# Attention with a learned position bias and a feed-forward layer on one core: bias rows 128 to 255 made per distance, constants in one load, two more places for the first layer

## The chip, the cores and the metric

The kernel runs on one core of a Trainium2 chip. The metric is the device time of one execution in microseconds (us). Engines are named as in the profile: PE is TensorE, DVE is VectorE, ACT is ScalarE, POOL is GpSimd, SP is SyncE, which here only issues transfers.

## What is computed

Batch 4, 8 heads, 576 positions, head size 64, all float32. To each head's scores a bias is added that a small network makes from the distance of the two positions; then softmax, the product with v, and a feed-forward layer (512 to 2048 to 512) over the 2304 tokens.

```python
scores = scale * np.matmul(q, k.transpose(0, 1, 3, 2))
rel = (pos[:, None] - pos[None, :]).astype(np.float32)
psi_rel = np.log1p(np.abs(rel))
psi_i = np.log1p(np.maximum(pos[:, None].astype(np.float32), 1.0))
x = (psi_rel / psi_i)[..., None]
h = np.maximum(x @ w1 + b1, 0.0)          # 32 hidden units
bias = h @ w2                             # 8 heads
scores = scores + bias.transpose(2, 0, 1)[None, :, :, :]
...                                       # softmax over the last axis
h = x @ w_in
g = h * np.clip(h + 3.0, 0.0, 6.0) / 6.0
out = g @ w_out
```

The bias doesn't depend on the batch, and the distance enters by its absolute value: row i of the bias needs h only for distances 0 to max(i, 575 - i).

## The kernel before

**The bias.** The 576 rows are made in 36 groups of 16 (`g`). In one group four rows of queries share a pass: 128 partitions are 4 rows times 32 hidden units, so a group has four first-layer passes (`z_group`, lines 1001 to 1022). A pass computes max(w1 * log-distance, -b1 * psi_i) or its Relu form, on ACT (line 1020) or on DVE (line 1016); groups below 16 alternate ACT and DVE, later ones have one ACT pass and three DVE passes. `T` holds the log-distances, already multiplied by w1 (lines 1243 to 1246, two DVE instructions). For groups below `EARLY = 16`, T is a table over signed offsets, and each pass reads a window of 576 columns of it. For later groups (`bias_far`) T is reloaded with one column per distance (`distances`, at tile 12), a pass reads only max(i, 575 - i) + 1 columns, and the row is unfolded on the way out of PSUM.

The second layer is a float32 matmul with `w2_sb` (line 1058; far groups line 1037), each pass on its own 32 of the output's partitions. ACT then scales by 1 / psi_i and adds a constant column of `cv_sb` (`bias_out`, line 1076): one instruction in an early group, two in a far one (the row to the right of the diagonal, and the mirrored row to its left). The group's rows go to a table in DRAM (line 1090, on ACT's queue), from which `load_bias` (line 645, on SP's queue) reads 128 rows for two heads at a time.

Passes of an even group write into `z_e`, of an odd group into `z_a`, in the first phase: each place is free again when its group's matmuls have read it. `z_a` also serves as the zeros for eight warm-up matmuls at the start (lines 1251 to 1255).

**The rest.** Around this, w_in and w_out are read as 64-bit floats in 1 MB pieces (line 396) and converted: ACT line 406, POOL line 407, DVE lines 414, 417 and 420 per piece, then the split in two halves, ACT line 285 and DVE line 302. Two buffers hold pieces of w_in, so a load waits until DVE line 420 has read the one before the last. The largest value of v is taken per 320 KB tile (DVE line 336). Score tiles follow as soon as their bias rows are in DRAM: scores on PE (line 683), with the bias added and the row's extreme taken on DVE (line 715), exp on ACT (line 726), transposes on PE (line 781). Feed-forward matmuls are lines 937 and 960.

**Order.** Every engine issues in program order, and `ISSUE` gives, for each engine, the order of its instructions as a list of their numbers in the order in which the kernel's Python creates them; what a list leaves out follows in that order. SP's numbers 0 to 7 are the constants' loads, then come w_in pieces, q/k tiles, v tiles and bias loads. All small loads, w_in, q, k, v and the bias loads stand in SP's one queue.

Of the kernel before, what the change touches and what calls it, by code (L numbers as in the profile page):

```python
# [1503 lines left out]
```

## Time and profile before

| what | value |
|---|---|
| median of 3 runs | 652.33 us (652.02 to 654.21) |
| the profiled execution | 653.62 us, of which its span 651.5 us |
| mean granted TensorE clock in it | 0.995 of full |
| busy share of the span: PE, PEld, ACT, DVE, POOL | 96%, 69%, 77%, 71%, 32% |

Busy time is what the profile counts for an engine's instructions; a share over the whole span is a mean over stages. Matmuls overlap, and their ends are modelled.

### The profile page before, as it was taken

What the parts mean: (1) busy time and instruction counts of PE and PEld (TensorE: products, weight loads), DVE (VectorE), ACT (ScalarE), POOL (GpSimd) and SP (SyncE); (2) the same over time, 40 slices, a digit from 0 to 9 for tenths busy, and PEclk for the clock granted to TensorE, in tenths of its full rate; (3) what the DMA queues carried; (4) which work ended last, traced back from release to release, by engine and by line L of the source; (5) the groups of instructions that cost most, each with busy time, mean ns of one, the idle gap of its engine ahead of it and who ended that gap; (6) DMA issues with size and microseconds to landing.
All of it is one profiled execution on the core that took longest, in us unless ns stands there. A gap on an engine that the chain in (4) does not pass through costs nothing.

```text
span 651.5 us, 14774 instructions
## 1 busy us (share of the span) xinstructions
PE 625.5 (96%) x5440; PEld 447.9 (69%) x5440; DVE 459.8 (71%) x1116; ACT 504.7 (77%) x993; POOL 208.3 (32%) x267
## 2 busy tenths in 40 slices
PE   6688998999999999999999999999999999999997
PEld 2225655666777777788888877777777777777775
DVE  4899999999858887676788667776677667821310
ACT  5898887999979989896799778976797678822620
POOL 0111115664223430452255125521444026300410
PEclk9889999999999999999999999999999999999999
DMA  8888788864679999999999999889878877640000
GB/s 278 317 322 298 283 310 318 308 232 140 163 205 247 215 274 194 264 251 234 257 259 248 203 209 180 176 177 205 173 142 187 181 168 139 113 81 21 1 12 31
DMA packets 176648, 130.57 MB, mean 200 GB/s; under 512 B 138304, under 2 KB 145728, under 8 KB 175552
## 3 DMA queue, kind: packets, MB, share of 16 engines
q1 hardware_dynamic: 166784, 114.14, 70.9%
q10 hardware_dynamic: 9792, 15.49, 8.5%
q8 instruction: 43, 0.70, 0.5%
q14 instruction: 29, 0.24, 0.1%
HBM read 77.54 MB, written 15.49 MB: 143 GB/s over the span
## 4 chain that ended last, share of the span: by engine, by line
PE 71%; DVE 4%; DMA 3%; ACT 1%; issue 0%; ACTq 0%; DVEq 0%; SPq 0%
PE o_ps L960 27%; PE h_ps L937 26%; PE s_ps L703 9%; PE pv_ps L868 6%; DMA at<-hl 2%; PE b_ps L1037 2%; DVE bt L715 1%; DMA wo<-in_w_out_dram 1%; DVE cu L420 1%; DVE cu L414 1%; ACT bt L726 0%; DVE wo L302 0%; PE pv_ps L822 0%; DVE cu L417 0%; ACT hl L285 0%
## 5 line engine op out<-in xcount | busy, mean ns | idle before, releaser
L937 PE MATMUL h_ps<-x,wi 128*128 128x256 f16 (+1 forms) x1536 | 205.7, 286 | 1.2 <-DVE x L1342 0.8
L960 PE MATMUL o_ps<-g,wo 128*128 128x256 f16 (+1 forms) x1536 | 198.8, 286 | 0.0
L937 PEld LDWEIGHTS <-wi 128*128 128x128 f16 x1536 | 146.6, 98 | 52.1 <-issue 15.8
L960 PEld LDWEIGHTS <-wo 128*128 128x128 f16 x1536 | 146.8, 98 | 46.4 <-issue 9.6
L916 POOL TENSOR_TENSOR g<-t,g 128x256 f16<-128x256 f32 (+1 forms) x128 | 105.0, 832 | 180.9 <-ACT g L914 173.9
L726 ACT ACTIVATE bt<-bt,sm 128x576 f32<-128x576 f32 x144 | 110.7, 770 | 31.0 <-DVE sm L715 30.6
L302 DVE SCALAR_TENSOR_TENSOR hl<-bt,sm,hl 128x576 f16<-128x576 f32 x112 | 95.2, 864 | 16.5 <-ACT hl L285 15.0
L285 ACT ACTIVATE hl<-bt,sm 128x576 f16<-128x576 f32 x112 | 84.0, 765 | 5.3 <-ACT bt L726 3.3
L920 DVE SCALAR_TENSOR_TENSOR t<-t,t,h_ps 128x320 f32<-128x320 f32 (+1 forms) x112 | 57.2, 516 | 40.2 <-ACT t L927 39.3
L564 POOL TENSOR_TENSOR qkl<-st,qkh 128x576 fp32r<-128x576 f32 (+2 forms) x48 | 53.1, 1124 | 90.3 <-ACT qkh L557 59.0
L914 ACT ACTIVATE g<-t 128x256 f16<-128x256 f32 (+1 forms) x128 | 54.9, 438 | 22.7 <-DVE t L920 22.3
L927 ACT ACTIVATE t<-h_ps,t,hr 128x320 f32<-128x320 f32 (+1 forms) x112 | 64.6, 586 | 8.4 <-PE h_ps L937 6.9
L715 DVE CUSTOM_DVE_ANT_0 bt<-s_ps,bt 128x576 f32<-128x576 f32 x88 | 64.8, 750 | 4.6 <-PE s_ps L703 4.4
L1016 DVE TENSOR_SCALAR z_e<-T,nbp 128x576 f32<-128x576 f32 (+17 forms) x76 | 36.5, 498 | 16.8 <-PE b_ps L1037 12.0
L734 DVE TENSOR_SCALAR sm<-sm 128x1 f32<-128x1 f32 x112 | 16.9, 151 | 44.0 <-ACT bt L726 43.7
L970 ACT ACTIVATE ot<-o_ps,os 128x256 f32<-128x256 f32 (+1 forms) x32 | 15.7, 491 | 38.4 <-PE o_ps L960 37.7
L1076 ACT ACTIVATE bo<-b_ps,cv_sb,isc 128x576 f32<-128x576 f32 (+36 forms) x60 | 36.7, 635 | 1.5 <-PE b_ps L1037 1.1
L715 DVE CUSTOM_DVE_ANT_0 bt<-s_ps,k 128x576 f32<-128x576 f32 x40 | 28.8, 752 | 5.9 <-PE s_ps L703 5.6
L407 POOL TENSOR_SCALAR w<-w 128x1024 f32<-128x1024 f32 x8 | 10.5, 1315 | 68.1 <-ACT wo L406 68.1
L868 PE MATMUL pv_ps<-at,vh 128*64 128x320 f16 (+1 forms) x432 | 32.0, 293 | 0.0
L1020 ACT ACTIVATE z_e<-T,bp 128x576 f32<-128x576 f32 (+17 forms) x36 | 24.9, 698 | 8.2 <-DVE bp L1247 3.4
L781 PE MATMUL t_ps<-eye_sb,bt 128*128 128x128 f32 x160 | 29.3, 280 | 1.1 <-ACT atf L784 0.5
(130 smaller groups left out, 845.0 us busy)
## 6 DMA issues: line engine op xcount, KB each, us to landing
bt<-bias SPq DMA_DIRECT2D x36, 576.0 KB, 5.6
w<-in_w_in_dram SPq DMA_DIRECT2D x8, 1024.0 KB, 6.6
vs<-in_vp_dram SPq DMA_DIRECT2D x24, 320.0 KB, 4.1
st<-in_qk_dram SPq DMA_DIRECT2D x16, 448.0 KB, 4.3
bias<-bo ACTq DMA_DIRECT2D x20, 295.5 KB, 4.4
wo<-in_w_out_dram SPq DMA_DIRECT2D x5, 1024.0 KB, 4.8
bias<-bo ACTq DMA_DIRECT2D x16, 288.0 KB, 4.3
bt<-bias SPq DMA_DIRECT2D x32, 144.0 KB, 3.3
```

The lines of the kernel that those rows point to most:

```text
L285: nc.scalar.activation(out=out, in_=full, func=AF.Copy, scale=scale)
L302: nc.vector.scalar_tensor_tensor(out=out, in0=full, scalar=scale, in1=high, op0=ALU.mult, op1=ALU.subtract)
L703: nc.tensor.matmul(out=s_t[n + j][:, a, 0:HALF], lhsT=w[q], rhs=m[rows, cs], start=(k == 0), stop=(k == 2),)
L715: nc.vector.tensor_tensor_reduce(out=halves(bt), in0=ps, in1=halves(src), op0=ALU.add, op1=ALU.min, scale=-0.125, scalar=3.0e38, accum_out ...
L726: nc.scalar.activation(out=bt, in_=bt, func=AF.Exp, scale=-1.0, bias=sm[:, 0:1], accum_out=total)
L868: nc.tensor.matmul(out=ps[64 * s:64 * s + 64, 0:n], lhsT=w[:, 128 * c + 64 * s:128 * c + 64 * s + 64], rhs=at[:, c, s * n:(s + 1) * n], st ...
L914: nc.scalar.activation(out=g[:, 0], in_=uu, func=AF.Copy)
L916: e.tensor_sub(out=g[:, 1], in0=uu, in1=g[:, 0])
L920: nc.vector.scalar_tensor_tensor(out=t_t[f], in0=t_t[f], scalar=cols(f)[2], in1=h_t.pop(f)[:, 0:n], op0=ALU.min, op1=ALU.mult,)
L927: nc.scalar.activation(out=t_t[f], in_=h_t[f][:, 0:n], func=AF.Relu, scale=cols(f)[0], bias=cols(f)[1],)
L937: nc.tensor.matmul(out=h_t[f][:, 0:n], lhsT=wi[:, a, c, f * 128:(f + 1) * 128], rhs=x[:, e, c], start=(k == 0), stop=(k == 3 * KC - 1),)
L960: nc.tensor.matmul(out=ops[:, 0:n], lhsT=wo[:, a, f, e * 128:(e + 1) * 128], rhs=g_t[f][:, r], start=(f == 0 and a == 0 and r == 0), stop= ...
```

## The change

- `EARLY` goes from 16 to 8, so groups 8 to 15 (rows 128 to 255) are made by `bias_far`, per distance. The DRAM table of rows 128 to 255 takes the shape that the tables of later rows have.
- T is no longer multiplied by w1. A pass does it: DVE's takes w1 and the bound as two scalars per partition, ACT's takes w1 as its scale. Two DVE instructions at the start and one POOL instruction in `distances` go.
- T's signed-offset part is columns 448 to 1147 and is loaded first; columns 0 to 447 hold distances from the start. `distances` loads only the other 128.
- w1, b1, psi, w2 and 1 / psi come in one block `cb`, in one load instead of five.
- `z_place`: groups 2, 3, 6, 7, 10 and 11 write their passes into two more places, in the buffers of the later transposed tiles (tags at0 and at1), so four places are in use up to group 11. The warm-up zeros move from `z_a` into a buffer of x.
- `s1` is 1: the constant columns `cv_sb` are made by six POOL memsets and one DVE multiplication, instead of a DVE memset and five DVE copies.
- All five issue lists are new. SP's starts: cb, T from 448 on, two v tiles, eye, a q/k tile, T up to 448, a q/k tile, w_in piece 0, a v tile, w_in piece 1, two q/k tiles, w_in pieces 2 and 3, the fourth v tile (number 18), the first bias load (12). DVE's starts: psi times b1, its negative, the zeros, three passes (groups 0, 1, 0), the maximum of the first v tile, a pass of group 3, `w2_sb` times 8 (number 4). PE's puts four of the eight warm-up matmuls behind the bias.

```diff
-EARLY = 16
+EARLY = 8
+ZMORE = 12
 LATE = 16 * EARLY
+FAR = 576 - LATE
...
-CFG = {... 's1': 0, ...}
+CFG = {... 's1': 1, ...}
...
 ISSUE = {
     "SP": """
-0-1 3 2 23 4 6 15 18 5 20 7 10 8 22 25 11-12 9 13-14 17 31 16 19 21 26 24 27-28 30 33 29 32 38 34 47
...
+0-1 11 14 2 6 3 7 4 16 5 8-10 13 18 12 19 17 15 22 21 20 26 23-24 27 25 29 28 30 43 32 31 35 33 47
...
+    cb = const.tile([128, 2 + S // 4 + 32 + NG], F32, name="cb")
+    w1_sb, b1_sb, bp = cb[:, 0:1], cb[:, 1:2], cb[:, 2:2 + S // 4]
+    w2_sb, isc = cb[:, 2 + S // 4:34 + S // 4], cb[:, 34 + S // 4:]
...
     def distances():
-        nc.sync.dma_start(out=T[:, 0:S], in_=dtab)
-        nc.gpsimd.tensor_scalar(
-            out=T[:, 0:S], in0=T[:, 0:S], scalar1=w1_sb, scalar2=1.0, op0=ALU.mult, op1=ALU.mult
-        )
+        nc.sync.dma_start(out=T[:, FAR:S], in_=dtab[:, FAR:S])
+
+    z_more = {}
+
+    def z_place(g):
+        if phase or g >= ZMORE or g % 4 < 2:
+            return z_a if phase == 0 and g % 2 else z_e
+        if g % 2 not in z_more:
+            t = at_p.tile([128, 5, 512], F32, tag=f"at{g % 2}", name="z_m")
+            t = t.rearrange("p a b -> p (a b)")[:, 0:4 * S]
+            z_more[g % 2] = t.rearrange("p (a b) -> p a b", a=2)
+        return z_more[g % 2]
...
-                z2 = (z_a if phase == 0 and g % 2 else z_e)[:, k // 2]
+                z2 = z_place(g)[:, k // 2]
...
-                    out=z, in0=src, scalar1=nbp[:, col], scalar2=None, op0=ALU.max
+                    out=z, in0=src, scalar1=w1_sb, scalar2=nbp[:, col], op0=ALU.mult, op1=ALU.max
...
-                nc.scalar.activation(out=z, in_=src, func=AF.Relu, bias=bp[:, col])
+                nc.scalar.activation(out=z, in_=src, func=AF.Relu, scale=w1_sb, bias=bp[:, col])
...
-    nc.sync.dma_start(out=T[:, 512:LT], in_=ltab[:, 512:LT])
-    nc.sync.dma_start(out=w1_sb, in_=w1c)
-    nc.sync.dma_start(out=b1_sb, in_=b1c)
-    (nc.scalar if cfg['s2'] else nc.sync).dma_start(out=bp, in_=psi)
-    nc.sync.dma_start(out=w2_sb, in_=w2b)
-    nc.sync.dma_start(out=isc, in_=ipsi)
+    nc.sync.dma_start(out=cb, in_=cblk)
+    nc.sync.dma_start(out=T[:, FAR:LT], in_=ltab[:, FAR:LT])
     nc.sync.dma_start(out=eye_sb, in_=eye)
-    nc.sync.dma_start(out=T[:, 0:512], in_=ltab[:, 0:512])
+    nc.sync.dma_start(out=T[:, 0:FAR], in_=dtab[:, 0:FAR])
...
-    for cs in (slice(512, LT), slice(0, 512)):
-        nc.vector.tensor_scalar(
-            out=T[:, cs], in0=T[:, cs], scalar1=w1_sb, scalar2=None, op0=ALU.mult
-        )
...
-        wz = z_a[:, 1, 0:S].bitcast(F16)
+        wz = x_p.tile([128, 2, KC, 256], F16, tag="x", name="wz")[:, 0].rearrange("p a b -> p (a b)")[:, 0:640]
```

## Rows read from the trace of the kernel before

**Rows 1.** Stretches: length, busy (xcount) of PE, PEld, DVE, ACT, POOL; clock, DMA share, GB/s.
```profile
5.00:53.00 48.00, 38.00 (x297) 15.00 (x297) 38.73 (x81) 41.38 (x57) 5.03 (x4) 0.93 0.89 315
53.00:150.00 97.00, 90.31 (x659) 58.17 (x661) 94.66 (x206) 83.00 (x154) 41.85 (x37) 1.00 0.80 294
150.00:200.00 50.00, 49.66 (x448) 35.88 (x447) 38.39 (x111) 44.21 (x88) 13.00 (x15) 1.00 0.65 171
200.00:600.00 400.00, 399.48 (x3689) 304.45 (x3688) 278.88 (x705) 318.08 (x663) 136.15 (x193) 1.00 0.91 192
```

**Rows 2.** The chain that ended last, around 160 us: start us, us, what.
```profile
159.54 0.76 DVE bt L715
...
160.36 0.44 PE t_ps L781 x2
```

**Rows 3.** DVE in order of time, the start: start us, us, what [idle before, releaser].
```profile
3.87 0.55 DVE L1244 TENSOR_SCALAR T<-T,w_sb 128x636 f32<-128x636 f32 x1 [3.87 <-DMA w_sb<-in_w1c_dram]
...
5.70 0.52 DVE L1016 TENSOR_SCALAR z_e<-T,nbp 128x576 f32<-128x576 f32 x1
```

**Rows 4.** ACT in order of time, the start.
```profile
5.42 1.44 ACT L1020 ACTIVATE z_e<-T,bp 128x576 f32<-128x576 f32 x2 [3.40 <-DVE bp L1247]
...
9.04 0.78 ACT L1020 ACTIVATE z_a<-T,bp 128x576 f32<-128x576 f32 x1 [1.51 <-PE w_ps L1255]
11.14 1.44 ACT L1020 ACTIVATE z_e<-T,bp 128x576 f32<-128x576 f32 x2 [1.32 <-PE b_ps L1058]
```

**Rows 5.** DMA issues of the first 60 us: median us from issue to landing at the end.
```profile
w<-in_w_in_dram SPq DMA_DIRECT2D x7, 1024.0 KB, 7.0
...
vf<-in_vp_dram SPq DMA_DIRECT2D x4, 320.0 KB, 5.6
T<-in_ltab_dram SPq DMA_DIRECT2D x1, 318.0 KB, 2.8
...
bp<-in_psi_dram SPq DMA_DIRECT2D x1, 72.0 KB, 2.4
```

**Rows 6.** Groups by line and shape, whole span: busy us, mean ns | idle before, releasers.
```profile
L1076 ACT ACTIVATE bo<-b_ps,cv_sb,isc 128x576 f32<-128x576 f32 x16 | 13.0, 824 | 0.3
L1020 ACT ACTIVATE z_e<-T,bp 128x576 f32<-128x576 f32 x17 | 12.8, 769 | 7.2 <-DVE bp L1247 3.4 <-PE b_ps L1058 2.9 <-ACT z_a L1020 0.8
...
L414 DVE TENSOR_SCALAR_CACHE_REDUCE cu<-cu 128x1024 f32<-128x1024 f32 x8 | 9.7, 1212 | 0.4 <-ACT cu L406 0.4
L1016 DVE TENSOR_SCALAR z_e<-T,nbp 128x576 f32<-128x576 f32 x19 | 9.4, 514 | 4.7 <-PE c_ps L1258 4.0 <-PE b_ps L1058 0.6
L1016 DVE TENSOR_SCALAR z_a<-T,nbp 128x576 f32<-128x576 f32 x16 | 8.1, 516 | 3.8 <-PE b_ps L1058 3.7
...
L1016 DVE TENSOR_SCALAR z_e<-T,nbp 128x384 f32<-128x384 f32 x3 | 1.2, 416 | 0.0
...
L1267 DVE COPY cv_sb<-c_ps 32x1 f32<-32x1 f32 x5 | 0.8, 157 | 0.2
...
L1076 ACT ACTIVATE bo<-b_ps,cv_sb,isc 128x64 f32<-128x64 f32 x2 | 0.8, 394 | 0.0
...
L1076 ACT ACTIVATE bo<-b_ps,cv_sb,isc 128x383 f32<-128x383 f32 x1 | 0.7, 667 | 0.0
...
L1020 ACT ACTIVATE z_e<-T,bp 128x384 f32<-128x384 f32 x1 | 0.6, 607 | 0.0
```

**Rows 7.** The second layer's matmuls by line and shape, whole span.
```profile
L1058 PE MATMUL b_ps<-z_e,w_sb 128*32 128x288 f32 x128 | 21.1, 487 | 7.9 <-DVE z_e L1016 6.7 <-ACT z_e L1020 1.1
...
L1037 PE MATMUL b_ps<-z_e,w_sb 128*32 128x448 f32 x8 | 1.0, 551 | 0.0
```

**Rows 8.** Two stretches, columns as in rows 1, around the fall of the clock.
```profile
20.00:25.00 5.00, 2.10 (x18) 0.73 (x22) 4.96 (x11) 4.15 (x7) 0.71 (x1) 0.95 1.01 402
25.00:28.00 3.00, 3.00 (x21) 1.01 (x14) 2.47 (x3) 1.74 (x4) 0.00 (x0) 0.51 0.42 154
```

**Rows 9.** PE in order of time: the first second-layer matmuls.
```profile
8.94 0.71 PE L1058 MATMUL b_ps<-z_e,w_sb 128*32 128x288 f32 x3
```

More of the change, by code (lines that the diff above doesn't have):

```diff
@@ L89 @@
+899 902 901 904 903 905-906 908 907 910 909 912 911 914 913
 """,
     "DVE": """
[L91 to L95 removed]
@@ new lines @@
+139-145 137 128 138 146-154 157-159 7 160-162 155-156 163 166 164-165 167-169 172 170 175-179 171
+180 173-174 181-184 190-191 185-186 192 187 193 188 194-196 211-215 189 216-217 197-210 225-234
+218-224 235-247 267 248-252 295 253-254 268-274 255 275-276 260-261 256-257 262 258 263-266 259
+277-278 281-289 279-280 310-317 290-294 318-323 296-298 303-304 299-300 305-306 301-302 307-309
+324-328 331-334 350 369 335 351 336-338 329-330 343-344 339 352-358 370-372 359 373-375 360 340
+345-346 376 341 347 342 377 348 378-380 349 361 388-397 362-363 398-401 364-365 402-403 414 366
@@ L197, in attention_moe_kernel @@
     vp: bass.AP,
-    w1c: bass.AP,
-    b1c: bass.AP,
-    w2b: bass.AP,
+    cblk: bass.AP,
     ltab: bass.AP,
     dtab: bass.AP,
-    psi: bass.AP,
-    ipsi: bass.AP,
     eye: bass.AP,
@@ L267, in attention_moe_kernel @@
     ]
-    b1_sb = const.tile([128, 1], F32, name="b1_sb")
-    w2_sb = const.tile([128, 32], F32, name="w2_sb")
+    cb = const.tile([128, 2 + S // 4 + 32 + NG], F32, name="cb")
+    w1_sb, b1_sb, bp = cb[:, 0:1], cb[:, 1:2], cb[:, 2:2 + S // 4]
+    w2_sb, isc = cb[:, 2 + S // 4:34 + S // 4], cb[:, 34 + S // 4:]
     tq = [const.tile([128, 2, 128], F32R, name=f"tq{r}") for r in range(2)]
@@ L1012, in z_group @@
                 nc.gpsimd.tensor_scalar(
-                    out=z, in0=src, scalar1=3.0e38, scalar2=nbp[:, col], op0=ALU.min, op1=ALU.max
+                    out=z, in0=src, scalar1=w1_sb, scalar2=nbp[:, col], op0=ALU.mult, op1=ALU.max
                 )
@@ L1016, in z_group @@
                 nc.vector.tensor_scalar(
-                    out=z, in0=src, scalar1=nbp[:, col], scalar2=None, op0=ALU.max
+                    out=z, in0=src, scalar1=w1_sb, scalar2=nbp[:, col], op0=ALU.mult, op1=ALU.max
                 )
             else:
-                nc.scalar.activation(out=z, in_=src, func=AF.Relu, bias=bp[:, col])
+                nc.scalar.activation(out=z, in_=src, func=AF.Relu, scale=w1_sb, bias=bp[:, col])
             zs.append(z)
@@ L1442, in attention_moe_kernel @@
     issue_in_order(tc, nc)
-_INS = ["qk", "qkd", "vp", "w1c", "b1c", "w2b", "ltab", "dtab", "psi", "ipsi", "eye", "w_in", "w_out"]
+_INS = ["qk", "qkd", "vp", "cblk", "ltab", "dtab", "eye", "w_in", "w_out"]
 def _layout(q, k, v, w1, b1, w2, moe_w_in, moe_w_out):
@@ L1477, in _layout @@
     d = {
-        "qk": qk, "qkd": qkd, "vp": vp, "w1c": w1c, "b1c": b1c, "w2b": w2b,
-        "ltab": ltab.astype(_np.float32), "dtab": dtab, "psi": psi, "ipsi": ipsi,
+        "qk": qk, "qkd": qkd, "vp": vp, "cblk": _np.concatenate([w1c, b1c, psi, w2b, ipsi], axis=1).astype(_np.float32),
+        "ltab": ltab.astype(_np.float32), "dtab": dtab,
         "eye": _np.eye(128, dtype=_np.float32),
```

237 lines of the change are left out of this document (110 added, 127 removed).

## The prediction

> **What bounds the kernel now.** I read the busy times by stretch first. From 200 to 600 us PE is busy 399.48 of 400 us, and from 150 to 200 us 49.66 of 50; from 53 to 150 us DVE is busy 94.66 of 97 us, ACT only 83.00; before 53 us neither is full, ACT with 41.38 of 48 us and DVE with 38.73 [rows 1]. The chain that ended last says the same: it goes back through PE to 160.36 us, and there steps over to DVE's bias-and-extreme instruction [rows 2]. So a microsecond saved early brings the PE-bound part forward by as much, if it lets DVE go on sooner. The change touches almost only the first 53 us, where all early bias groups are made. The question is what holds that stretch: engine work or waits.
>
> Then the start in order of time, and the groups by shape with what ended the idle time before them. DVE's first instruction, T times w1, waits for the load of w1 until 3.87 us, and its first pass runs at 5.70 [rows 3]. ACT's first pass runs at 5.42; then it stands 1.51 us before the second pass into z_a, which the warm-up matmuls still read, and 1.32 us for z_e [rows 4]. In all, ACT's passes wait 2.9 us on the matmuls for z_e besides that 1.51, DVE's 4.0 and 0.6 us for z_e and 3.7 us for z_a [rows 6]. Two places for the first layer are too few there.
>
> **The change part by part.** The sum is for the time at which the bias groups are done, ACT and DVE apart.
>
> *Start.* The first z pass needs T, psi times b1 and, on DVE, its negative. Now T lands before 3.87 us and b1 after. With one block of 107 KB first (its nearest rows: 72 KB in 2.4 us, 318 KB in 2.8 [rows 5]) and T second, I estimate the first passes at 4.1 us: 1.3 us sooner on ACT (from 5.42), 1.6 on DVE (from 5.70). The scaling of T goes; its first part, 0.55 us [rows 3], ran while psi was still missing; the second has 512 columns instead of 636, so about 0.5 us of DVE work counts.
>
> *Groups 8 to 15.* The widths go from 576 to 448, 432 and so on to 336, 392 on average. On DVE 16 passes of 0.515 us become about 0.42 (the row for 384 columns: 0.416): 16 x 0.097 = 1.55 us less. On ACT 16 passes of 0.77 become 0.61 (384 columns: 0.607): 2.5 us less. But each group's way out is two instructions instead of one: the right part, 392 columns on average, near the row for 383 (0.667), the mirrored one, 199, between 64 columns (0.394) and 383, so 0.51. That is 1.18 us in place of 0.824, 8 x 0.35 = 2.8 us more [rows 6]. ACT ends with 0.3 us more work. On PE one bank of matmuls per group replaces two: 21.1 us for eight groups (128 records), 2.6 us each, become about 1.0 (8 records) [rows 7]. Even at half the clock that is 2.0, so I charge PE nothing.
>
> *w1 inside the pass.* ACT's scaled form already exists in the way out; I take 0. For DVE no row shows a wide pass with two scalars per partition. The nearest is the same instruction with one: from 384 to 576 columns 0.416 to 0.514 us, 0.51 ns a column [rows 6]. The other bound is about one column a cycle, as line 414 with two operations and an accumulation: 1.212 us for 1024 columns, so some 0.80 us for 576 [rows 6]. I take the first, since only the second scalar differs, and keep the second as a rival.
>
> The Trainium skill (VectorE: DVE Perf Modes, The perf-mode tier table) gives float32 tensor_scalar between SBUF operands a double rate, as an operation and without a word on the number of scalars. By it the sum stays as it is; by the row of line 414 it would be the third rival's. The 0.51 ns a column of the one-scalar pass agrees with the page; for two scalars no run here shows it.
>
> *Constant columns.* Five copies of 0.157 us and a memset leave DVE, one small multiplication comes [rows 6]: 0.7 us less. The six POOL memsets lie where POOL has nothing to do.
>
> *Places.* With four up to group 11, the wait on the warm-ups and most waits on matmuls should go. ACT's total is 1.5 + 2.9 = 4.4 us in the listed rows; I take 4.0. The least is 1.5 (the warm-ups alone), the most 4.4 and small gaps, 5.5. DVE's total is 4.0 + 0.6 + 3.7 = 8.3; I take half, since DVE also waits for ACT's halves of the same groups.
>
> *Moved steps.* Three could cost. First, DVE scales w2_sb only behind the maximum of the first v tile, so the first matmul hangs on a 320 KB load (5.6 us in the median [rows 5]): issued third, right behind T, it is there at 6 to 7.5 us, and the matmul starts at 7 to 9 us instead of 8.94 [rows 9]. With four places ACT has eight passes (6 us) to make meanwhile, so this is hidden. Second, SP's queue has the fourth v tile and the first bias load behind w_in piece 3, which waits until DVE line 420 has read piece 1. The bias load stood there before too; the v tile was loaded early. Its maximum stands on DVE ahead of the first score tiles. DVE has eight passes and three 1.2 us conversions, some 7 us, between; a v tile landing 5.6 us after its issue, behind 1 MB that takes 7.0 [rows 5], comes 0 to 3 us late if I am unlucky. I take 0 and keep 3 for the range. Third, `distances` loads a quarter and needs no POOL pass; that lies beside other work, 0. The SP lists after that differ in ways of which the rows show no price; bounds 1 us either way.
>
> *Sum.* ACT: 1.3 + 4.0 - 0.3 = 5.0 us sooner. DVE: 1.6 + 0.5 + 1.55 + 0.7 + 4.1 = 8.5 us sooner. The groups need both, so 5.0 holds up to group 15; behind that DVE is the bound and can use part of its further 3.5. I take 6.0, nearer to ACT's, since DVE's next work needs ACT's conversions. Everything behind is the same work in about the same order. The profiled execution took 653.62 us, 1.3 above the median; against itself it would become 647.6. From the median of 652.33 I predict 646.3 us. The bounds: ACT's least 1.3 + 1.5 - 0.3 = 2.5, less a late v tile, and DVE's full 8.5 and 1 more: 642.8 to 652.8.
>
> **The rivals.**
> (1) *A new wait takes half.* The late v tile, or loads that land no sooner, hold DVE while ACT is ahead. For it: the DMA engines are busy 0.89 of 5 to 53 us [rows 1], and the new queue asks for the same bytes. Against: w_in pieces 0 and 1 are issued earlier. The time: 652.33 - 6 + 3 = 649.3.
> (2) *Nothing arrives.* The groups are done sooner, but the first score tiles and the w_in pieces come when they came, because the transfers set them. For it the same 0.89 share; against it, DVE's full stretch from 53 us starts with a queue of work that is ready. Time 652.3, within 0.3% either way, which is about 2 us and what a measurement of this kernel can tell from no change.
> (3) *The two-scalar pass is half as fast on DVE.* Price: groups 0 to 7, 16 x 0.29 = 4.6 us more; groups 8 to 15, 384 columns at about 0.61 instead of 0.515, 16 x 0.10 = 1.6; less the 0.5 and 0.7 of the other edits and 0.6 of the start: 4.4 us more DVE work in a front that DVE then sets. It decides once a 576-column pass takes over some 0.7 us, for then DVE's 8.5 us are gone. Time 656.7. For it: the only wide two-operation rows run at that rate. Against: they also accumulate, and the pass has one tensor input as before.
>
> **How the numbers follow.** Forecast 0.57, rival 1 0.20, rival 2 0.13, rival 3 0.10. Rival 1 is faster by 3 us in the middle, and about a quarter of it falls within 0.3%: so faster 0.72, same 0.17, slower 0.11 (rival 3 and a little of rival 2). The range reaches from the forecast's lower bound, a little widened, 642.0, to 652.8, which takes in rival 1 and most of rival 2 and leaves out rival 3. The likeliest case alone is 642.8 to 650.
>
> **What would show it.** Right: the first passes near 4.1 us; line 1016 at about 0.51 us for 576 columns, 0.42 for 384; almost no wait of ACT's passes on matmuls before group 12; the last pass of group 15 and the step of the chain from DVE to PE each some 6 us sooner, the latter near 154 us [rows 2]. Wrong: a 576-column pass of 0.7 us or more (rival 3); DVE standing before the maximum of the fourth v tile (rival 1); DVE's stretch from the last group on with new idle time before the conversions of w_in (rival 2). The clock is the other thing to look at: PE was busy 2.10 of 5 us, and then 25 to 28 us ran at 0.51, 1.2 GHz [rows 8]. With fewer columns it may stay there longer, which hurts only if the first score matmuls fall into it.

## The result, and the profile after

The changed kernel takes 656.79 us (median of 6 runs, 656.59 to 660.49), the kernel before, run beside it, 652.56 (6 runs, 651.45 to 655.66): a ratio of 1.0079, with a 95% interval of 1.0057 to 1.0100. It is 4.2 us slower by the medians (5.2 by the ratio) where 6.0 us faster was forecast. The profiled execution took 656.62 us, its span is 654.8. All ratios below are to the kernel before on the same chip, with 95% intervals. Three executions were slow and count in no median and no ratio below, two of e1 (662.83 and 3485.43 us, the latter the profiled one, so of e1 only the times are read) and one of e2 (1830.27 us).

By stretches, the columns those of [rows 1]; the last line is the stretch from 150 to 160 us of the kernel before:

```profile
5.00:53.00 48.00, 30.24 (x223) 11.04 (x222) 37.48 (x74) 45.01 (x68) 4.68 (x4) 0.89 0.86 302
53.00:150.00 97.00, 89.44 (x667) 58.68 (x668) 93.01 (x203) 82.09 (x152) 35.06 (x36) 1.00 0.82 294
150.00:160.00 10.00, 7.75 (x53) 5.61 (x51) 9.76 (x28) 8.29 (x19) 5.56 (x6) 0.83 0.13 42
160.00:200.00 40.00, 39.03 (x354) 28.60 (x355) 31.69 (x79) 31.77 (x61) 6.70 (x8) 1.00 0.76 208
200.00:600.00 400.00, 399.50 (x3705) 305.61 (x3704) 282.85 (x710) 321.58 (x670) 135.06 (x193) 1.00 0.90 192
```

```profile
150.00:160.00 10.00, 9.80 (x84) 6.71 (x82) 9.75 (x32) 10.00 (x19) 3.54 (x4) 1.00 0.32 108
```

ACT has 45.01 us of work before 53 us instead of 41.38 [rows 1]: more, where the sum had it nearly even (0.8 us of it is the activation table's load, which stood ahead of 5 us before). PE has 30.24 instead of 38.00, at a lower granted clock (0.89 for 0.93). From 150 to 160 us, where PE had been busy 9.80 us at full clock, it is busy 7.75 us at a clock of 0.83. After 200 us PE is as full as before (399.50 and 399.48 of 400 us): DVE's step on the score tile that stood at 198.8 us is 3.2 us late, and the whole span is 3.3 us longer.

The start, first ACT's table load in the kernel before, then ACT, DVE and PE of the changed kernel in order of time:

```profile
0.74 1.28 ACT L1020 ACT_TABLE_LOAD   x1 [0.74 <-PEq L1492]
```

```profile
4.51 1.28 ACT L1020 ACT_TABLE_LOAD   x1 [4.51 <-DMA T<-in_ltab_dram]
5.80 0.87 ACT L1020 ACTIVATE z_a<-T,cb 128x576 f32<-128x576 f32 x1
...
4.52 0.58 DVE L1016 TENSOR_SCALAR z_e<-T,cb,nbp 128x576 f32<-128x576 f32 x1 [0.75 <-DMA T<-in_ltab_dram]
...
9.00 0.69 PE L1058 MATMUL b_ps<-z_e,cb 128*32 128x288 f32 x2 [3.29 <-ACT z_e L1020]
```

DVE begins 1.2 us sooner than in [rows 3], ACT 0.4 us later than in [rows 4]: the activation table (ACT_TABLE_LOAD in these rows), loaded at 0.74 us in the kernel before, now stands behind the wait for T and takes 1.28 us of ACT's path. PE's first second-layer matmul is no earlier than in [rows 9], because its pass is the fourth in ACT's new order.

The groups by shape that answer to [rows 6]:

```profile
L1020 ACT ACTIVATE z_m<-T,cb 128x576 f32<-128x576 f32 x8 | 6.7, 860 | 0.0
L1076 ACT ACTIVATE bo<-b_ps,cv_sb,cb 128x576 f32<-128x576 f32 x8 | 6.4, 827 | 0.3 <-PE b_ps L1058 0.3
...
L1016 DVE TENSOR_SCALAR z_m<-T,cb,nbp 128x576 f32<-128x576 f32 x8 | 4.5, 574 | 4.3 <-PE b_ps L1058 4.3
L1020 ACT ACTIVATE z_e<-T,cb 128x576 f32<-128x576 f32 x5 | 4.2, 857 | 1.1 <-PE b_ps L1058 1.1
L1016 DVE TENSOR_SCALAR z_e<-T,cb,nbp 128x576 f32<-128x576 f32 x7 | 3.9, 574 | 3.4 <-PE b_ps L1058 2.0 <-DMA T<-in_ltab_dram 0.8 <-PE b_ps L1037 0.6
...
L1016 DVE TENSOR_SCALAR z_e<-T,cb,nbp 128x384 f32<-128x384 f32 x5 | 2.4, 474 | 0.9 <-PE b_ps L1037 0.9
...
L1020 ACT ACTIVATE z_e<-T,cb 128x384 f32<-128x384 f32 x3 | 2.2, 717 | 0.0
```

Each pass with w1 inside is dearer on both engines: on DVE 574 ns instead of 514 at 576 columns and 474 instead of 416 at 384, on ACT 860 instead of 769 and 717 instead of 607 (626 in e2, below). ACT's waits on matmuls are nearly gone (1.1 us left); of DVE's 8.3 us some 6.3 stand (4.3 and 2.0).

Between 53 and 150 us DVE is busy 1.65 us less than in [rows 1]; part of it is a longer wait for a load: ACT waits for a piece of w_out, and DVE for ACT. The first line is the kernel before, where ACT waited 1.46 us there:

```profile
91.69 2.19 ACT L406 ACTIVATE cu<-wo 128x1024 f32<-128x1024 f32 x2 [1.46 <-DMA wo<-in_w_out_dram]
```

```profile
93.84 2.16 ACT L398 ACTIVATE cu<-wo 128x1024 f32<-128x1024 f32 x2 [2.60 <-DMA wo<-in_w_out_dram]
...
95.00 1.22 DVE L406 TENSOR_SCALAR_CACHE_REDUCE cu<-cu 128x1024 f32<-128x1024 f32 x1 [1.29 <-ACT cu L398]
```

So far the traces. Adding up DVE's instruction durations up to 53 us by the function that issues them gives, before and after, 44.25 and 43.34 us; less the passes (16.49, 17.37) and the constants, scalings and clears (3.24, 1.38), DVE's other work done by 53 us is 24.5 and 24.6 us. The first 53 us won nothing, and what follows lost. (Each kernel has one trace, and executions of one kernel differ by several us, so small differences between two traces show where time goes and not how much.)

### The profile page after: what moved, and what is told of

The parts are those of the page before. It is cut to its first block, busy times and chain, and to the rows that moved or that the text cites. A ratio compares the mean times of both kernels' runs of the same rounds, so it can differ in the third digit from the quotient of the medians.

```text
span 654.8 us, 14633 instructions
## 1 busy us (share of the span) xinstructions
PE 618.8 (94%) x5376; PEld 446.9 (68%) x5376; DVE 464.9 (71%) x1109; ACT 507.6 (78%) x1001; POOL 200.4 (31%) x272
## 4 chain that ended last, share of the span: by engine, by line
PE 63%; ACT 1%; DVE 1%; issue 0%; ACTq 0%
PE o_ps L952 25%; PE h_ps L929 23%; PE s_ps L695 8%; PE pv_ps L860 6%; PE b_ps L1037 1%; ACT bo L1076 0%; ACT z_e L1020 0%; ACT hl L277 0%; DVE z_e L1016 0%; ACT ot L962 0%; DVE t L912 0%; DVE vl L294 0%; ACT g L906 0%; DVE hl L294 0%; DVE bt L707 0%
## 5 line engine op out<-in xcount | busy, mean ns | idle before, releaser
L929 PE MATMUL h_ps<-x,wi 128*128 128x256 f16 (+1 forms) x1536 | 203.1, 287 | 1.1 <-DVE sm L707 1.1
L952 PE MATMUL o_ps<-g,wo 128*128 128x256 f16 (+1 forms) x1536 | 196.5, 286 | 0.5 <-ACT g L277 0.4
L908 POOL TENSOR_TENSOR g<-t,g 128x256 f16<-128x256 f32 (+1 forms) x128 | 100.2, 794 | 183.8 <-ACT g L906 174.9
L1076 ACT ACTIVATE bo<-b_ps,cv_sb,cb 128x576 f32<-128x576 f32 (+27 forms) x68 | 38.5, 608 | 4.0 <-PE b_ps L1037 3.6
L1016 DVE TENSOR_SCALAR z_e<-T,cb,nbp 128x576 f32<-128x576 f32 (+17 forms) x70 | 36.5, 541 | 7.1 <-PE b_ps L1037 4.2
L695 PE MATMUL s_ps<-qkh 64*128 64x288 f32 x192 | 26.5, 345 | 1.6 <-DVE sm L707 1.0
```

Source lines behind the costliest of these rows:

```text
L695: nc.tensor.matmul(out=s_t[n + j][:, a, 0:HALF], lhsT=w[q], rhs=m[rows, cs], start=(k == 0), stop=(k == 2),)
L908: e.tensor_sub(out=g[:, 1], in0=uu, in1=g[:, 0])
L929: nc.tensor.matmul(out=h_t[f][:, 0:n], lhsT=wi[:, a, c, f * 128:(f + 1) * 128], rhs=x[:, e, c], start=(k == 0), stop=(k == 3 * KC - 1),)
L952: nc.tensor.matmul(out=ops[:, 0:n], lhsT=wo[:, a, f, e * 128:(e + 1) * 128], rhs=g_t[f][:, r], start=(f == 0 and a == 0 and r == 0), stop= ...
```

## The experiments

Three theories: PRICE (the new instructions are dearer than taken), START and ORDER (the first ten microseconds, or the new issue orders as a whole, lose the time), and, later, CLOCK (PE has too little to do, its granted clock falls, and that costs). In the variants that keep "old orders", every instruction stands where it or its counterpart stood in the kernel before; "w1 ahead" means that T is multiplied by w1 before the passes, as in the kernel before. Every run's mean granted clock is recorded; "clock" in the table is its mean over the runs that count. A thousandth of the time is 0.65 us. A difference of two ratios is given with an interval (±) that takes the two intervals as independent.

| kernel | median us | ratio to before | interval | clock |
|---|---|---|---|---|
| changed kernel | 656.79 | 1.0079 | 1.0057 to 1.0100 | 0.988 |
| e1 changed code, old orders | 653.54 | 1.0025 | 0.9994 to 1.0057 | 0.993 |
| e2 changed, w1 left out | 654.31 | 1.0028 | 0.9997 to 1.0058 | 0.989 |
| e3 before, w1 inside | 655.24 | 1.0058 | 1.0036 to 1.0080 | 0.995 |
| e4 before, groups 8 to 15 per distance | 654.23 | 1.0027 | 1.0006 to 1.0048 | 0.993 |
| e5 changed, start mended | 654.89 | 1.0043 | 1.0013 to 1.0074 | 0.986 |
| e6 changed, far matmuls twice | 656.17 | 1.0045 | 1.0022 to 1.0068 | 0.994 |
| e7 changed code, old orders, w1 ahead | 652.21 | 1.0000 | 0.9972 to 1.0028 | 0.993 |
| e8 before, constants in one load | 653.50 | 1.0011 | 0.9986 to 1.0035 | 0.994 |
| e9 e7, far matmuls twice | 652.11 | 1.0009 | 0.9984 to 1.0035 | 0.995 |
| e10 e8 and two more places | 651.48 | 0.9979 | 0.9951 to 1.0006 | 0.996 |
| e11 changed, start mended, w1 ahead | 652.06 | 0.9998 | 0.9974 to 1.0021 | 0.986 |
| e12 e10, smaller first load of T | 651.99 | 1.0004 | 0.9986 to 1.0023 | 0.995 |
| e13 changed, table early alone | 656.22 | 1.0067 | 1.0045 to 1.0089 | 0.988 |
| e14 changed, starting order alone | 656.99 | 1.0088 | 1.0059 to 1.0117 | 0.985 |
| e15 e11, far matmuls twice | 652.79 | 0.9995 | 0.9965 to 1.0025 | 0.992 |
| e16 e11, groups 8 to 15 per row | 653.84 | 1.0013 | 0.9987 to 1.0038 | 0.991 |

The kernel before, run beside each group of them, has 0.996 to 0.997 in that column.

**The price of w1 inside.**

e2, w1 in no pass (and nowhere else: that part of the computation is left out):

```diff
-                    out=z, in0=src, scalar1=w1_sb, scalar2=nbp[:, col], op0=ALU.mult, op1=ALU.max
+                    out=z, in0=src, scalar1=nbp[:, col], scalar2=None, op0=ALU.max
...
-                nc.scalar.activation(out=z, in_=src, func=AF.Relu, scale=w1_sb, bias=bp[:, col])
+                nc.scalar.activation(out=z, in_=src, func=AF.Relu, bias=bp[:, col])
```

> The changed kernel with the multiplication by w1 left out of all 144 first-layer passes (it is done nowhere, so that part of the computation is missing); orders and everything else as in the changed kernel. Passes should be back at 0.515 (DVE, 576 columns) and 0.77 us (ACT, 576 columns). PRICE expects 652.5 to 654 us: 32 ACT passes of the first 16 groups give back about 3 us, 32 DVE passes 1.8 us. ORDER expects 655.5 to 657 us, because what the passes give back falls into waits that the order makes.

e3, the reverse in the kernel before, its three scalings of T taken out (DVE's two shown, POOL's not):

```diff
-                    out=z, in0=src, scalar1=nbp[:, col], scalar2=None, op0=ALU.max
+                    out=z, in0=src, scalar1=w1_sb, scalar2=nbp[:, col], op0=ALU.mult, op1=ALU.max
...
-                nc.scalar.activation(out=z, in_=src, func=AF.Relu, bias=bp[:, col])
+                nc.scalar.activation(out=z, in_=src, func=AF.Relu, scale=w1_sb, bias=bp[:, col])
...
-        nc.vector.tensor_scalar(
-            out=T[:, cs], in0=T[:, cs], scalar1=w1_sb, scalar2=None, op0=ALU.mult
-        )
```

> The kernel before with one part of the change alone: w1 inside the passes, and the scalings of T (two on DVE, one on POOL) gone; its orders stay. PRICE expects 653.5 to 656 us: ACT +3 us and DVE +1.8 us in the first 53 us against 1.3 us that DVE starts earlier. ORDER expects 651 to 652.5 us: the first 53 us have room for it on both engines.

e1, the changed code in the old orders (only the lists in ISSUE differ; here the front of ACT's):

```diff
-3 12 1 0 4 7 11 15 8 5 20 19 16 6 2 9 13 24 29 17 28 10 32 25 14 33 21
+0-1 3-4 7-8 5 12 11 6 9 15 13 16 19 2 14 20 17 24 21 28 10 18 22 25 29
```

> The changed kernel's instructions, but issued in the orders of the kernel before (new instructions stand where their counterparts stood). Theory PRICE (the change's own instructions cost too much: the pass with w1 inside is 0.06 us longer on DVE and 0.09 to 0.11 us longer on ACT, the activation table is loaded 1.3 us too late) expects no better than the changed kernel, 656 us or more, since the old order makes no use of the two more places. Theory ORDER (the new issue orders move work from the unfilled first 53 us into the stretch where DVE is full) expects about the time of the kernel before or a little less, 649 to 652.5 us, and the stretch from 53 to 160 us losing nothing.

The groups by shape of e2:

```profile
L1028 ACT ACTIVATE z_m<-T,cb 128x576 f32<-128x576 f32 x8 | 6.0, 770 | 0.0
L1024 DVE TENSOR_SCALAR z_m<-T,nbp 128x576 f32<-128x576 f32 x8 | 4.0, 518 | 4.7 <-PE b_ps L1066 4.7
...
L1024 DVE TENSOR_SCALAR z_e<-T,nbp 128x384 f32<-128x384 f32 x5 | 2.1, 415 | 0.9 <-PE b_ps L1045 0.9
...
L1028 ACT ACTIVATE z_e<-T,cb 128x384 f32<-128x384 f32 x3 | 1.9, 626 | 0.0
```

Without w1 the passes are back at their old durations (on ACT at 384 columns nearly, 626 for 607), so little else made them longer. Four pairs differ by w1 alone or nearly so (in e11 and e7 T is scaled instead): e2 against the changed kernel (5.1 thousandths, 3.3 us), e3 against the kernel before (5.8, 3.8 us), e11 against e5 (4.5, 2.9 us) and e7 against e1 (2.5, 1.6 us). PRICE stands: 1.6 to 3.8 us, 2.9 in the mean; e3's time lies in the range that it expected, e2's just above (654.31 for 652.5 to 654). e3's interval is clear of 1 by itself; of the other differences the first (±3.7) and the third (±3.9) are clear of 0, the last (±4.2) is not. In the trace of e2 the first score tile comes 2.0 us sooner than in the changed kernel, and 2.2 us are left at 150 us: the price falls in the 64 passes before 53 us. The 60 later DVE passes run behind 150 us, beside a full PE, and no cost of theirs is seen: at the end the trace of e2 is 1.2 us ahead of that of the changed kernel.

e1 came between the two expectations: it gives back 5.4 thousandths (±3.8) of the changed kernel, so the new orders do cost, though w1 still stands inside the passes. What of the orders costs is the next question.

**The start.** e5 puts a one-column activation at ACT's front and reorders the beginning; e13 has only the activation, e14 only the order.

```diff
+    tl = const.tile([128, 2], F32, name="tl")
+    nc.gpsimd.memset(tl[:, 0:1], 0.0)
+    nc.scalar.activation(out=tl[:, 1:2], in_=tl[:, 0:1], func=AF.Relu)
     nc.sync.dma_start(out=cb, in_=cblk)
```

The order of e5 and e14, the fronts of ACT's, DVE's and PE's lists as they are in e14:

```diff
-3 12 1 0 4 7 11 15 8 5 20 19 16 6 2 9 13 24 29 17 28 10 32 25 14 33 21
+0-1 3-4 12 7 11 15 8 5 20 19 16 6 2 9 13 24 29 17 28 10 32 25 14 33 21
...
-2-3 5 7 10 8 40 14 4 13 46 1 9 11-12 15 6 22 16 24 18 17 25 19 23 55 2
+2-3 5 4 7 10 8 40 14 13 46 1 9 11-12 15 6 22 16 24 18 17 25 19 23 55 2
...
-0-3 12-13 8-10 20 14-17 21 18 22-23 28 11 24-26 19 29-32 36 33 27 34 3
+0-7 12-13 8-10 20 14-17 21 18 22-23 28 11 24-26 19 29-32 36 33 27 34 3
```

> The changed kernel with its start put right and nothing else: a one-column activation without a DMA behind it stands first on ACT (so that the table is loaded at once), ACT's first four passes stand in the order in which PE wants them, DVE scales w2 ahead of its first pass, and PE's eight warm-ups stand together at the front. Theory START (about 3 us of the forecast were lost in the first ten microseconds: table load behind T, PE waiting until 9.0 us and then at 1.2 GHz) expects the first second-layer matmul near 7.5 us, and 1.5 to 4 us less than the changed kernel. Rival: what is saved before 10 us is lost again in the waits that the order makes before 53 us; 0 to 0.7 us less.

> The changed kernel with the one-column activation first on ACT and nothing else: the table is loaded at 0.74 us instead of 4.51 us, ACT's first pass should stand at 4.7 us (5.80 in the changed kernel). If ACT's late start is what e5 won, 1 to 1.9 us less than the changed kernel; if not, 0 to 0.5 us less, because PE's first matmul is held by the place of its pass in ACT's order.

> The other half of e5 alone: ACT's first four passes in PE's order, w2 scaled ahead of the first DVE pass, all eight warm-ups at PE's front; the table load stays late. If PE's start (first second-layer matmul at 9.00 us, then at 1.2 GHz to about 13.5 us) is what e5 won, 1 to 1.9 us less than the changed kernel, with the first matmul near 8 us; if the table is, 0 to 0.5 us.

ACT and PE in order of time, e5 (its profiled execution, 660.39 us, is the slowest of the twelve; only its start is read):

```profile
0.74 1.28 ACT L1229 ACT_TABLE_LOAD   x1 [0.74 <-PEq L1491]
...
4.71 1.62 ACT L1027 ACTIVATE z_e<-T,cb 128x576 f32<-128x576 f32 x2 [2.47 <-DMA T<-in_ltab_dram]
...
7.28 0.63 PE L1065 MATMUL b_ps<-z_e,cb 128*32 128x288 f32 x2
...
7.74 0.41 PE L1065 MATMUL b_ps<-z_e,cb 128*32 128x288 f32 x2
```

PE in e13, then in e14:

```profile
7.81 0.69 PE L1066 MATMUL b_ps<-z_e,cb 128*32 128x288 f32 x2 [2.14 <-ACT z_e L1028]
...
8.29 0.69 PE L1066 MATMUL b_ps<-z_e,cb 128*32 128x288 f32 x2
```

```profile
7.29 0.70 PE L1065 MATMUL b_ps<-z_e,cb 128*32 128x288 f32 x2
...
7.77 0.69 PE L1065 MATMUL b_ps<-z_e,cb 128*32 128x288 f32 x2
```

Together they give 3.6 thousandths, 2.3 us, with an interval (±3.7) that just holds 0. The same step with w1 outside the passes, from e2 to e11 (below), gives 3.0, and the mean of the two, 3.3 ± 2.7, is clear of 0. Alone, e13 (1.2 thousandths faster) and e14 (0.9 slower), with six runs each, can't be told from the changed kernel. The rows suggest why the two may need each other; no run shows it. The first of these matmuls that takes under 0.5 us instead of 0.69 stands at 13.97 us in the changed kernel, at 12.79 in e13, 9.81 in e14 and 7.74 in e5, where the passes come right behind eight warm-ups without a gap; it stands at 10.86 in the kernel before, but at 12.89 in e8, which is level with that one. (The expectations speak of 1.2 GHz there; the profile's clock column says 1.00 in these microseconds, so the durations alone are the evidence.)

**Old orders, and one part at a time.** e4, from the kernel before (the other load and the scalings of T follow, not shown):

```diff
-EARLY = 16
+EARLY = 8
 LATE = 16 * EARLY
+FAR = 576 - LATE
...
-    nc.sync.dma_start(out=T[:, 512:LT], in_=ltab[:, 512:LT])
+    nc.sync.dma_start(out=T[:, FAR:LT], in_=ltab[:, FAR:LT])
```

> The kernel before with another part alone: groups 8 to 15 made per distance (shorter passes, four second-layer matmuls instead of eight, two ACT instructions on the way out instead of one), T still scaled ahead, its orders kept. Both theories expect the forecast's terms to hold: DVE 1.5 us less, ACT about 0.3 us more, so 650.5 to 652.5 us. A rival, that the two-part way out delays the stores and so the first score tiles, expects 653 us or more.

e7 is the changed code in the old orders, with the passes of e2 and T scaled again (by POOL in `distances` too, not shown):

```diff
+    for cs in (slice(FAR, LT), slice(0, FAR)):
+        nc.vector.tensor_scalar(
+            out=T[:, cs], in0=T[:, cs], scalar1=w1_sb, scalar2=None, op0=ALU.mult
+        )
```

> The changed kernel's code with w1 multiplied into T ahead of the passes again (two scalings on DVE, one on POOL) and the old issue orders; constants in one load, per-distance groups 8 to 15 and the two places stay. PRICE (w1 inside the passes costs 2.3 to 2.7 us) and the run in the old order (level with the kernel before) together expect 2 to 3 us less than the kernel before at the same granted clock, 650 to 651 us. If the two do not add up, because the first 53 us are bound by something else (the loads of w_in and v), it comes out level with the kernel before.

e8 is e7 with EARLY = 16 and ZMORE = 0, e10 is e7 with EARLY = 16 alone, and e12 is e10 with this, and with T's other loads and its scalings as in the kernel before:

```diff
-    nc.sync.dma_start(out=T[:, FAR:LT], in_=ltab[:, FAR:LT])
+    nc.sync.dma_start(out=T[:, 512:LT], in_=ltab[:, 512:LT])
```

> The kernel before with the third part alone: small constants in one load, the mask columns on POOL with one DVE multiplication, warm-up operand in another tile; w1 ahead of the passes, groups 8 to 15 per row, two places, old orders. Its first DVE pass should stand near 5.1 us (5.70 before). If the start is worth what the forecast took (DVE 0.7 us of columns and about 0.6 us earlier), 650.5 to 652 us; if the start is hidden, level with the kernel before; a later start on ACT by the table load would show as 653 us or more.

> The run with the constants part alone (e8) and the two more places beside it: groups 8 to 15 per row with their eight matmuls, w1 ahead, old orders. If the places are what made e7 better than the sum of its parts (e4 1.2 us slower and e8 level, but both together with the places level or 0.7 us faster), it comes out 1 to 3 us below the kernel before, 650 to 652 us. If the old order, which was made for fewer places, does not use them, level with e8, 653 us.

> e10 (the kernel before with constants in one load and two more places, groups 8 to 15 per row, w1 ahead, old orders) with T loaded and scaled as in the kernel before, so that the first load is 636 columns instead of 828. In e10 the first DVE pass stood 0.2 us ahead of the kernel before although the constants were there at 2.8 us; with the smaller load it should stand near 4.9 us. If an early microsecond counts, 0.3 to 0.6 us less than e10, 650.8 to 651.2 us, and clear of the kernel before; if the sixth load of w_in, which waits for its buffer, sets the time there, the same as e10.

e4 is 1.8 us slower by its ratio and just clear of no change: the per-distance form alone wins nothing. The time is that of the rival in its expectation, but the rival's reason, late first score tiles, is not in the trace: DVE's step on the first one stands 0.4 us sooner than in the kernel before (these two lines), and the time is lost later.

```profile
45.24 0.76 DVE L721 CUSTOM_DVE_ANT_0 bt<-s_ps,bt 128x576 f32<-128x576 f32 x1 [0.86 <-PE b_ps L1043]
```

```profile
45.66 0.76 DVE L715 CUSTOM_DVE_ANT_0 bt<-s_ps,bt 128x576 f32<-128x576 f32 x1
```

e8 is level. e7 and e10 are not separable from the kernel before; e10 has the lowest ratio, and its interval still holds 1. e12's first DVE pass stood at 5.03 us, where e10's stood at 5.49, and it was no better than e10. All parts but w1 together (e7) come to nothing, although PE's first second-layer matmul of e7 stands at 5.79 us, 3.15 before that of [rows 9].

**Where an early microsecond goes.** In e7 the conversion of w_in is 7.1 us ahead of the kernel before at 43 us, the first score tile 4.2, the steps at 52 us 3.1, those from 70 us on 1.7. The rest stays: this trace (651.34 us) ends some 2 us ahead of that of the kernel before (653.62), no more than two executions of one kernel differ. Stretches of e7, then DVE and ACT in order of time; the last line is ACT's wait in the kernel before:

```profile
30.00:35.00 5.00, 2.70 (x18) 0.61 (x16) 4.45 (x14) 5.00 (x9) 1.19 (x1) 1.00 0.85 260
35.00:40.00 5.00, 5.00 (x14) 1.17 (x12) 3.49 (x5) 4.10 (x7) 1.51 (x1) 0.60 0.95 328
40.00:45.00 5.00, 5.00 (x15) 1.58 (x14) 2.90 (x8) 2.72 (x6) 0.00 (x0) 0.50 0.94 372
...
41.45 0.76 DVE L719 CUSTOM_DVE_ANT_0 bt<-s_ps,bt 128x576 f32<-128x576 f32 x1 [2.96 <-PE s_ps L687]
...
57.37 1.12 ACT L410 ACTIVATE wo<-w 128x1024 f32<-128x1024 f32 x1 [2.48 <-DMA w<-in_w_in_dram]
```

```profile
59.84 1.14 ACT L406 ACTIVATE wo<-w 128x1024 f32<-128x1024 f32 x1 [1.89 <-DMA w<-in_w_in_dram]
```

Two things take it. PE, busy 2.70 of 5 us, then runs at 0.60 and 0.50 (1.2 GHz) just when the first score matmuls come; it is full, and DVE waits 2.96 us. And a later piece of w_in is not there: its load waits on SP for a buffer that DVE frees, so ACT waits 2.48 us (1.89 in the kernel before) and DVE behind it.

**The clock.** e6, e9 and e15 issue the four matmuls of each of groups 8 to 15 twice into the same place, so that PE has as many to do as before.

```diff
             for k, z in enumerate(zs):
-                nc.tensor.matmul(
-                    out=pss[a][32 * k:32 * k + 32, 0:hi - lo], lhsT=w2_sb, rhs=z[:, lo:hi]
-                )
+                for _ in range(2 if g < 16 else 1):
+                    nc.tensor.matmul(
+                        out=pss[a][32 * k:32 * k + 32, 0:hi - lo], lhsT=w2_sb, rhs=z[:, lo:hi]
+                    )
```

> The changed kernel with the four second-layer matmuls of each of groups 8 to 15 issued twice into the same place (32 matmuls more, about 0.3 to 0.6 us each, as many as the change had removed); the output stays. Theory CLOCK (the changed kernel's PE has so little to do between 24 and 53 us that its granted clock falls, and the time follows the mean granted clock) expects the granted clock of 30 to 53 us to rise from 0.85 to 0.95 or more, and 1 to 3 us less than the changed kernel although PE does more. The rival, that the clock follows the waits and costs nothing there, expects the same time or 1 to 4 us more, for the doubled matmuls stand in the chain of the bias rows.

> The run with the changed code, w1 ahead and old orders (e7), and the four second-layer matmuls of groups 8 to 15 issued twice into the same place, as in e6. In e7 the bias rows were 7 us ahead of the kernel before at 44 us and only 3 us ahead at 52 us: PE was 2.70 us busy in 30 to 35 us, then its granted clock stood at 0.60 and 0.50 from 35 to 45 us with PE full, and DVE waited 2.96 us for the first score tile. CLOCK expects the granted clock of 35 to 45 us near 1.00 and 1.5 to 3 us less than e7, 649 to 650.7 us. The rival, that the doubled matmuls cost in the chain what the clock gives, expects the same as e7 or more, 652 to 654 us.

> The mended changed kernel (e11: its own orders, start put right, w1 ahead) with the four second-layer matmuls of groups 8 to 15 issued twice, as in e6 and e9. e11 was level with the kernel before although its bias rows were 5.9 us ahead at 52 us, and its mean granted clock was the lowest of all runs (0.979 to 0.992, against 0.995 and more). CLOCK expects a mean clock of 0.991 or more and 1 to 2.5 us less than e11: 649.5 to 651 us. The rival (a filled PE costs what the clock gives, as in e6 and e9) expects 652 us, level with e11.

A stretch of e6, then the same of the changed kernel, whose clock there is 0.85:

```profile
30.00:53.00 23.00, 18.25 (x139) 7.38 (x135) 17.86 (x34) 20.23 (x34) 2.23 (x2) 0.93 0.87 298
```

```profile
30.00:53.00 23.00, 13.73 (x77) 4.61 (x74) 19.47 (x41) 21.70 (x38) 2.22 (x2) 0.85 0.91 309
```

The same stretches and waits in e9:

```profile
30.00:35.00 5.00, 4.39 (x34) 1.42 (x34) 4.00 (x11) 5.00 (x9) 1.21 (x1) 1.00 0.84 275
35.00:40.00 5.00, 4.67 (x20) 1.65 (x20) 4.16 (x8) 4.84 (x8) 1.47 (x1) 1.00 1.00 343
40.00:45.00 5.00, 5.00 (x33) 2.00 (x36) 3.19 (x8) 3.19 (x7) 0.00 (x0) 1.00 0.95 366
...
40.99 0.76 DVE L720 CUSTOM_DVE_ANT_0 bt<-s_ps,bt 128x576 f32<-128x576 f32 x1 [1.83 <-PE s_ps L688]
...
56.58 1.12 ACT L411 ACTIVATE wo<-w 128x1024 f32<-128x1024 f32 x1 [2.99 <-DMA w<-in_w_in_dram]
```

In all three the clock rises, as CLOCK expects (0.988 to 0.994, 0.993 to 0.995, 0.986 to 0.992), though from 30 to 53 us of e6 only to 0.93 where 0.95 was expected. The time does not follow: e9 and e15 are level with e7 and e11, and e6's 3.4 thousandths (±3.2) are at the edge of the noise; the three pairs together give 0.9 ± 2.1 thousandths in favour of the doubled matmuls. In e9 DVE's wait on the score matmuls is shorter (1.83 us) and ACT's wait for w_in longer (2.99): of what the clock gives, the next wait takes a part; what the doubled matmuls take was not measured. Fewer matmuls lower the clock; that filling PE pays is not shown.

**Both mended.** e11 joins the edits of e5 and e7 in the new orders; e16 is e11 with EARLY = 16.

> The changed kernel in its own orders with both mended: the start as in e5 and w1 multiplied into T ahead of the passes as in e7. If the two losses add up (1.9 us for the start, 2.5 us for w1 inside) it takes 652 to 653 us, level with the kernel before and with e7, and then nothing else in the new orders costs. If the new orders hold a further loss between 53 and 160 us (PE 0.83 of the clock at 150 to 160 us, work of DVE left over), it stays at 653.5 to 655 us.

> The mended changed kernel (e11) with groups 8 to 15 per row again (eight matmuls, one way out, passes of 576 columns). It takes back the part that e4 found to cost 0 to 2 us in the old orders. If the per-distance form earns nothing because it leaves PE idle while ACT's way out takes 3 us more, this comes out at or below e11: 650 to 652 us, with a mean clock above 0.99. If its shorter passes (DVE 1.5 us, ACT 2.5 us) are part of e11's lead at 52 us, 653 to 654.5 us.

e11 is level with the kernel before, and with e7, which has the same code, but for the one-column activation, in the old orders: beyond the start, nothing of the new orders is seen to cost. That is what the sum of the two losses demanded: w1 2.9 and start 2.3 us make 5.2, and from the changed kernel to e11 it is 8.1 thousandths, 5.3 us, with intervals that do not touch. The changed kernel, e2, e5 and e11 are w1 in or out by start old or mended; over this square w1 is worth 4.8 thousandths (±2.7) and the start 3.3 (±2.7). Taking the per-distance form back (e16) changes nothing that can be told. e11's DVE has 29.3 us of its other work done at 53 us, 4.8 more than the kernel before; e8, which is level too, has 28.1. e11's stretches, then ACT and DVE in order of time:

```profile
53.00:150.00 97.00, 88.28 (x657) 57.40 (x658) 91.67 (x201) 81.09 (x152) 36.47 (x38) 0.98 0.79 282
150.00:160.00 10.00, 8.20 (x63) 5.71 (x60) 9.76 (x32) 9.49 (x19) 3.72 (x5) 1.00 0.26 94
...
89.36 2.16 ACT L405 ACTIVATE cu<-wo 128x1024 f32<-128x1024 f32 x2 [2.45 <-DMA wo<-in_w_out_dram]
...
90.53 1.22 DVE L413 TENSOR_SCALAR_CACHE_REDUCE cu<-cu 128x1024 f32<-128x1024 f32 x1 [1.17 <-ACT cu L405]
...
99.93 0.42 DVE L852 TENSOR_TENSOR xr<-pv_ps,xr 128x256 f32<-128x256 f32 x1 [1.51 <-ACT xr L844]
```

DVE is busy 91.67 of 97 us there, 94.66 in [rows 1]: 3.0 of the 4.8 us go in idle time. The lines show the longest pieces, behind the load of w_out (ACT waits 2.45 us, 1.46 in the kernel before) and behind ACT. DVE's step on the score tile at 152 us and the end of this trace are 1.1 and 1.2 us ahead; the median is level.

## Why the prediction was wrong

*w1 inside the pass* is the step that failed first. On ACT "scaled form already exists in the way out; I take 0" priced the existence and not the duration: a pass got 0.09 to 0.11 us longer, 32 passes about 3 us, and ACT was the engine that set the sum. Edits that take w1 out or put it in show the cost of both engines together: 3.1 us in the square above, 3.8 in e3; the engines were not tried apart. The hint stood in [rows 6]: 576 columns took 824 ns with a scale and 769 without. The Trainium skill (ScalarE: Activation LUTs, What ACT_TABLE_LOAD costs) would have priced it: it puts about 93 ns on each per-partition pointer operand of an ACTIVATE, and 860 against 769 ns agrees. On DVE "0.51 ns a column" held: from 384 to 576 columns the two-scalar pass takes 474 and 574 ns, 0.52 ns a column. What was missed is a fixed 0.06 us a pass, 1.9 us for the 32 early ones.

*Start.* "First passes at 4.1 us" came to 4.52 on DVE, since T landed later, and to 5.80 on ACT. That the table load would move behind the new wait was not in the forecast. "The matmul starts at 7 to 9 us" held at its last moment, 9.00, but not by the v tile: by ACT's order, which the forecast had not priced at all. *Constant columns* and the scaling of T gave what was taken and more: with the clears they fall from 3.24 to 1.38 us of DVE's work, 1.9 less for 1.2.

*Groups 8 to 15.* The way out was right (ACT's `bo` work up to 53 us rose from 13.18 to 16.15 us, 3.0 against 2.8 forecast). The shorter passes were right too, as e4 shows, which has them without w1 inside: up to 53 us they fall from 16.49 to 14.90 us on DVE and from 25.90 to 23.40 on ACT, 1.6 and 2.5 less, as forecast. In the changed kernel w1's price ate them: 607 became 717 ns at 384 columns instead of staying. "I charge PE nothing" holds for PE's time; that fewer matmuls lower the granted clock was named at the end of the forecast and is what e7's first score tiles show.

*Places.* ACT's waits fell by 3.3 us where 4.0 was taken, DVE's by about 2.0 where 4.1 was taken.

*Sum.* The premise "a microsecond saved early brings the PE-bound part forward by as much, if it lets DVE go on sooner" failed, with w1 and start mended too. The eight kernels with w1 ahead whose first second-layer matmul stands 1.5 to 3.2 us sooner (5.74 to 7.39 us in e7 to e12, e15 and e16, 8.94 before) lie between 0.9979 and 1.0013, and no interval of theirs leaves out 1. The condition was met until 53 us (4.8 us more DVE work done in e11) and then broken; the traces of e7 and e11 show by what, the next waits: pieces of w_in and w_out whose buffers DVE itself frees, and ACT. That these waits alone took it is read from one trace each and not shown by an edit.

*The first two rivals.* The late v tile was there, but DVE waited 0.32 us for it and not 3:

```profile
40.06 0.82 DVE L328 TENSOR_REDUCE vparts<-vf 128x1 f32<-128x640 f32 x1 [0.32 <-DMA vf<-in_vp_dram]
```

The second, "nothing arrives", has the time of the mended kernels, and the changed kernel pays for w1 and the start on top of it. Its reason is only half there: the first score tiles did come sooner (4.2 us in e7, 5.3 in e11), and the lead went behind them.

*The third rival* gave 656.7 us, the measured time, by a mechanism that was not there: its bound was a DVE pass of over 0.7 us, and 0.574 was measured. The time that agrees does not speak for the reason.

*Open.* How much of the 4.2 us goes through the clock. Over 33 runs of the kernel before beside e1 to e4, the 11 with a mean granted clock of 0.997 or more took 649.95 to 651.41 us, the 17 at 0.994 or 0.995 took 652.04 to 656.25, the 5 below 654.12 to 657.30: the same instructions, about 3 us for 0.004. The changed kernel's clock is 0.007 to 0.009 lower. So the clock may carry most of what PRICE and START do, as their later link, or stand beside them; e11, with the changed kernel's clock and the time of the kernel before, speaks against the clock alone. All recorded runs (on several chips), taken at one mean clock, go a step further. At 0.989 to 0.992 the changed kernel's four runs took 656.59 to 656.94 us and 20 of the kernel before 655.2 in the mean (653.01 to 658.37): there some 1.5 us of the loss are left, and the rest goes with the lower clock. At 0.997 or more e3's six took 653.49 to 655.04 us, 59 of the kernel before 650.9 in the mean: there w1 inside costs 3.4 us at an equal mean clock. But e1's four at that clock, with w1 inside too, took 650.37 to 650.87. This compares runs and is no experiment; whether a low clock makes a run long or long waits make the clock low stays open.

## What to carry to other kernels

A factor moved into an instruction is not free because the form exists: compare two rows of the same width with and without the operand, and multiply by the count on the engine that sets the sum. Before counting an early saving at the end, follow it through the next waits in the trace (a load whose buffer the saved engine frees, an engine that had been just in time), for what follows may have no room for it. Issue orders made for one set of durations are part of the change: the same code differed by 5.4 thousandths between two orders.

## What the hardware showed that was not expected

- A second operation with a second per-partition scalar costs a DVE tensor_scalar 0.06 us at either width (514 to 574 ns at 576 columns, 416 to 474 at 384); operation and scalar were not tried apart.
- The activation table's load (1.28 us) waits with the first activation: at 0.74 us in the kernel before, at 4.51 us in the changed kernel, whose first pass waits for a DMA itself, and again at 0.74 us in e5, where a one-column activation that needs no DMA stands in front.
- Taking matmuls away lowered the granted clock of what came next: in e7 PE was busy 2.70 of 5 us and then full at 0.60 and 0.50 for ten; with the doubled matmuls (e9) it was busy 4.39 of 5 and stayed at 1.00. The mean clock over all runs went the same way in the three pairs with doubled matmuls.
